# Zero matmuls ahead of the first km units instead of the first k'v, in a fused attention and channel-mix kernel with a new instruction table

## Chip, core and metric

The kernel runs on one core of one Trainium2 chip. The metric is the time of one execution on the device in microseconds (us), median of three runs. Beside it stands one profiled execution, whose trace gives the start and length of every instruction.

## The reference

Linear attention without softmax, a norm per head, and then a channel mix of RWKV kind (8 batches, 8 heads, 576 tokens, head width 64, model width 512, hidden width 1024):

```python
kv  = einsum('bhsd,bhse->bhde', k, v)          # k'v: one 64x64 matrix for each head
out = einsum('bhsd,bhde->bhse', q, kv)
out = out / sqrt(mean(out * out, -1) + 1e-6) * g_norm
x   = out.transpose(0, 2, 1, 3).reshape(B, S, 512)
xk  = mu_k * x + (1 - mu_k) * x_prev            # x_prev: the token before
xr  = mu_r * x + (1 - mu_r) * x_prev
k   = relu(xk @ w_k);  v = (k * k) @ w_v
return sigmoid(xr @ w_r) * v                    # [8, 576, 512], float32
```

## The kernel before

Everything runs in bf16 with sums in float32. The work of a batch is a string of units, each a handful of matmuls with what moves their result out of PSUM. The units are written out by hand in a table, `ORDER` (lines 18 to 113): eight periods of words, which the last loop of the kernel issues one after the other. A word is the unit's name, its arguments, a prime if VectorE instead of ScalarE does the elementwise part, and after `=` the PSUM banks (0 to 7) that the unit takes. Since each engine works through its own instructions in the order of issue, the table sets the order on every engine; an engine waits where an operand isn't there yet.

The units that the change and the prediction speak of:

- `wm.n`: n zero matmuls of 512 columns into a bank that nobody reads (`warm`, line 256). Twelve more are issued ahead of the table (line 629).
- `cast`: k and v of batch 0, first half of the heads, from float32. `kvc`, `qtc`, `uc`, `sqc`, `msc`, `rsc`, `mcc` (and `kvco`, `qtco`, which move out): batch 0 in a transposed form: k'v, q turned, q times k'v, its square, the mean over a head by a matmul, the root, the product that gives x.
- `kvh`, `qt`, `uh`, `sqh`, `redh`, `rsh`, `mulh`, `xh`, `x0h`: the same for batch 1 in halves of the heads; here the mean is a VectorE reduction and x is turned back by PE.
- `kv`, `qt`, `u`, `sq`, `red`, `nw` (eight small Newton steps on VectorE), `mul`, `x` and `x0` (the flips by PE), `xo` and `x0o` (their move out): batches 2 to 7.
- `wrap`, `dif`, `sc`, `add`, `fu`: x minus the token before, times mu, plus x; `add.b.0.*` gives xk, `add.b.1.*` gives xr.
- `Ka`, `Kz`, `Kp` and `K`: km, that is xk @ w_k and the relu. `Ka` and `Kz` are the two halves of the heads of batch 0's tokens 256 to 575, one block of 128 hidden columns each; `Kp.0.1.n` its tokens 0 to 255. `ks`, `ksp`: the squares.
- `R`: xr @ w_r and the sigmoid, for 128 tokens. `V` (or `Vq`, a quarter): the product with w_v for 128 tokens. `fin`: sigmoid times that, and the store. `L`: the last tile in two halves.
- `ld.i.b`: load of k, v or q (i = 0, 1, 2) of batch b, issued from GpSimd's queue. There is one buffer for each of the three, so the load of a batch's k waits until the k'v of the batch before has read it. The stores go out from SP's queue.

w_k comes in two halves of 512 hidden columns (`load_w`, line 195), issued ahead of the table on GpSimd's queue together with batch 1's inputs, w_v and w_r; `Ka.0.0` to `Ka.0.3` need the first half only.

Of the kernel before, what the change touches and what calls it, by code (L numbers as in the profile page):

```python
# [29 lines left out]
    mulh.1.0.0 mulh.1.1.0 Kp.0.1.2=5 Vq.0.3.0=4 Vq.0.3.1 mulh.2.0.0 rsh.5.9.0 mulh.0.0.0 Vq.0.2.0=3 Vq.0.2.1  # L30
    mulh.0.1.0 xh.0.2.0=51 xho.0.2.0.0 qt.1.1=20 qto.1.1.0 xho.0.2.0.1' qto.1.1.1' xh.2.2.0=76 xho.2.2.0.0
    x0h.0=51 x0ho.0.0 kvh.1=20 kvho.1.1 xho.2.2.0.1' ksp.0.1.4.8' kvho.1.0' Vq.0.1.0=6 x0ho.0.1' add.0.1.1
    uh.0.1=75 uh.1.1=02 sqh.0.0.1 sqh.0.1.1 redh.5.9.1 sqh.1.1.1 uh.2.1=1 sqh.2.0.1 Vq.0.1.1 sqh.1.0.1
    redh.0.5.1 Vq.0.3.2 rsh.5.9.1 rsh.0.5.1 mulh.0.1.1 mulh.0.0.1 Vq.0.2.2 Vq.0.2.3 mulh.1.0.1 Vq.0.1.2 tab
    Vq.0.3.3 Vq.0.0.0=5 mulh.1.1.1 mulh.2.0.1 Vq.0.0.1 xh.2.2.1=70 xho.2.2.1.0 xh.0.2.1=21 xho.0.2.1.1'
    xho.2.2.1.1' wrap.1 Vq.0.0.2 Vq.0.0.3 dif.1.384.576 sc.1.0.0.384.576' x0h.1=71 sc.1.0.2.384.576' x0ho.1.0
    x0ho.1.1' xho.0.2.1.0 dif.1.0.384 sc.1.0.1.384.576 sc.1.0.3.384.576 sc.1.0.2.0.384' R.0.0=0 sc.1.1.3'
    sc.1.0.0.0.384' ld.0.2 R.0.1=7 adda.1.0.384.576 R.0.2=2 sc.1.0.1.0.384' add.1.0.0.0.384 ld.1.2 Vq.0.1.3
    fin.0.0 fin.0.1 fin.0.2 R.0.3=1 sc.1.0.3.0.384 fin.0.3 add.1.0.1.0.384 sc.1.1.2
# [15 lines left out]
    K.2.0.0=7 K.2.0.1=2 K.2.1.0=5 K.2.1.1=7 K.2.2.0=2 K.2.2.1=5 K.2.3.0=7 K.2.3.1=2 K.2.4.0=5 red.3.5.9 nw.3.0.1
    add.2.1.1 K.2.4.1=7 nw.3.1.2 ks.2.0' K.2.5.0'=2 K.2.5.1=5 ks.2.1 K.2.6.0=7 K.2.6.1=2 nw.3.2.3 nw.3.3.4
    nw.3.4.5 nw.3.5.6 nw.3.6.7 ks.2.6 nw.3.7.8 mul.3.0.1 ld.1.4 ld.2.4 mul.3.2.0 mul.3.1.1 ks.2.4' ks.2.3 ks.2.2
    R.2.0=5 R.2.1=7 mul.3.0.0 V.1.8.0=2 V.1.8.1 mul.3.1.0 fin.1.8 K.2.7.0=3 qt.4.0=46 qto.4.0.0' x0.3=15
    x.3.0.4=70 xo.3.0.4.1' qt.4.1=23 x0o.3.0 ks.2.5' x0o.3.1 wrap.3 qto.4.0.1' kv.4=14 xo.3.0.4.0 K.2.7.1=5
# [7 lines left out]
    nw.4.7.8 mul.4.1.1 K.3.5.0=0 K.3.5.1=6 K.3.6.0=5 ld.2.5 mul.4.0.0 mul.4.2.0 add.3.1.1 mul.4.1.0 K.3.6.1=3
    ks.3.3 ks.3.6' ks.3.4 qt.5.1=04 kv.5=76 kvo.5.0' kvo.5.1 qto.5.1.1' qt.5.0=53 qto.5.0.0 add.3.1.0 qto.5.0.1'
    qto.5.1.0 ks.3.0 V.2.3.0=1 K.3.7.0=7 K.3.7.1=4 V.2.3.1 ks.3.2' R.3.4=6 ks.3.1' mul.4.0.1 fin.2.3 x0.4=53
    x.4.0.4=07 x0o.4.0' x0o.4.1 u.5.1=42 u.5.0=15 ks.3.7' xo.4.0.4.0 xo.4.0.4.1' wrap.4 ks.3.5' sq.5.1.0 dif.4  # L70
    u.5.2=6 sc.4.1.3' sc.4.0.2' ld.0.6 sc.4.0.3' R.3.5=3 V.3.5.0=7 sq.5.2.0 add.4.0.1 sc.4.0.1' sq.5.1.1
# [7 lines left out]
    V.3.7.0=5 ks.4.0' V.3.7.1 fin.3.7 ks.4.3 x0.5=34 x.5.0.4=27 x0o.5.0 x0o.5.1' kv.6=61 qt.6.0=03 xo.5.0.4.1'
    xo.5.0.4.0 kvo.6.0 wrap.5 kvo.6.1' qt.6.1=54 qto.6.1.1 qto.6.0.0 qto.6.1.0' dif.5 sc.5.0.3' K.4.6.0'=7  # L80
    qto.6.0.1 K.4.6.1=2 K.4.7.0=1 K.4.7.1=6 u.6.1=54 sc.5.0.2' sc.5.0.0 sc.5.0.1' ks.4.4' add.5.0.0 u.6.0=03
    u.6.2=2 sq.6.1.1 sq.6.0.1 sq.6.1.0 ld.0.7 add.5.0.1 sq.6.2.0 sc.5.1.0' V.3.8.0=1 V.3.8.1 sq.6.0.0 fin.3.8
    red.6.0.5 red.6.5.9 nw.6.0.1 nw.6.1.2 nw.6.2.3 nw.6.3.4 nw.6.4.5 ks.4.5 nw.6.5.6 nw.6.6.7 nw.6.7.8 R.4.0=7
# [3 lines left out]
    K.5.0.0=7 K.5.0.1=6 mul.6.2.0 mul.6.1.1 sc.5.1.1 K.5.1.0=1 K.5.1.1=7 R.4.3=6 ks.4.1 add.5.1.0 K.5.2.0=1
    K.5.2.1=7 K.5.3.0=2 K.5.3.1=6 K.5.4.0=4 ks.4.6 V.4.0.0=1 mul.6.1.0 mul.6.0.1 x0.6=72 x0o.6.1 mul.6.0.0
    ks.4.7' x0o.6.0' ld.1.7 kv.7=56 ld.2.7 kvo.7.1 sc.5.1.3' x.6.0.4=34 qt.7.1=07 qto.7.1.1 qt.7.0=26 qto.7.0.1'
    qto.7.0.0' V.4.0.1 sc.5.1.2' V.4.1.0=7 V.4.1.1 add.5.1.1 xo.6.0.4.1 wrap.6 xo.6.0.4.0 dif.6 kvo.7.0'  # L90
# [665 lines left out]
```

## Time and profile before

| | us |
|---|---|
| median of 3 runs | 204.84 (204.07, 204.84, 206.48) |
| the profiled execution, its time | 205.55 |
| the profiled execution, its span | 203.7 |
| PE (TensorE) busy in the span | 194.9 |
| VectorE (DVE) busy | 163.0 |
| ScalarE (ACT) busy | 135.8 |

The span runs from the first to the last instruction that the profile shows; about 1.9 us of the execution lie outside it. Busy time of PE counts matmuls, and their ends are modelled, so a busy PE is not a PE at its peak; PEld is the loading of weights beside it. PEclk is the clock that was granted to PE, 1.00 being full. In rows of the timeline the first number is the start, the second the length, and the bracket at the end says how long the engine sat idle before and what it waited for.

### The profile page before, as it was taken

How to read it: one execution, taken by the hardware profiler on the slowest of the kernel's cores; microseconds unless marked ns; L12 is line 12 of the kernel's file. 1: busy time of each engine (PE TensorE's matmuls, PEld its weight loads, DVE VectorE, ACT ScalarE, POOL GpSimd, SP SyncE). 2: the span in 40 equal slices, each digit the busy share in tenths (PEclk: the TensorE clock that was granted, in tenths of full speed). 3: DMA queues.
4: the chain of work that ended last, by engine and by line, in shares of the span. 5: the costliest groups of instructions: out<-in, count | busy, mean ns of one | idle time of the engine just before them, and what ended most of it. 6: DMA issues, size and time to landing. Idle time of an engine off the chain costs nothing.

```text
span 203.7 us, 6357 instructions
## 1 busy us (share of the span) xinstructions
PE 194.9 (96%) x2684; PEld 117.3 (58%) x2684; DVE 163.0 (80%) x359; ACT 135.8 (67%) x282; POOL 27.3 (13%) x44
## 2 busy tenths in 40 slices
PE   7969999999979999999999999999999999999992
...
DVE  1389899899969899979999999978898897467151
...
PEclk9996999999999999999999999999999999999999
DMA  6999999989989902995698339900440060006664
GB/s 214 214 205 206 202 205 171 204 156 178 247 115 206 282 5 55 139 214 154 98 226 172 69 56 188 211 5 3 105 103 3 0 156 3 0 0 156 138 141 136
DMA packets 21424, 27.22 MB, mean 134 GB/s; under 512 B 1804, under 2 KB 16404, under 8 KB 21396
## 3 DMA queue, kind: packets, MB, share of 16 engines
...
q8 instruction: 21, 0.34, 0.7%
q10 hardware_dynamic: 320, 0.39, 0.6%
q14 instruction: 7, 0.06, 0.1%
...
## 4 chain that ended last, share of the span: by engine, by line
PE 71%; DMA 21%; issue 3%; POOL 2%; DVE 0%; POOLq 0%
PE ps_v L605 27%; PE ps_km L573 25%; PE ps_r L595 11%; DMA in_k<-in_k_dram 7%; DMA in_q<-in_q_dram 6%; DMA in_v<-in_v_dram 5%; DMA q<-in_q_dram 3%; PE ps_qt L299 2%; PE ps_u L321 2%; PE ps_kv L285 2%; PE ps_x L377 2%; PE ps_v L613 1%; POOL q L185 0%; POOL wv_sb L204 0%; POOL in_k L193 0%
## 5 line engine op out<-in xcount | busy, mean ns | idle before, releaser
L605 PE MATMUL ps_v<-wv_sb,sqk 128*128 128x512 bf16 x280 | 66.1, 379 | 0.0
L573 PE MATMUL ps_km<-xk,wk_sb 128*128 128x288 bf16 (+3 forms) x480 | 63.4, 285 | 0.0
L573 PEld LDWEIGHTS <-wk_sb 128*128 128x128 bf16 x480 | 45.9, 98 | 15.8
L565 ACT ACTIVATE rt<-ps_km 128x288 bf16<-128x288 f32 (+3 forms) x92 | 37.4, 431 | 15.0 <-PE ps_km L573 9.5
L605 PEld LDWEIGHTS <-sqk 128*128 128x128 bf16 x280 | 26.5, 98 | 28.5
L598 ACT ACTIVATE sig<-ps_r 128x512 bf16<-128x512 f32 x36 | 21.0, 603 | 21.5 <-PE ps_r L595 21.3
L595 PE MATMUL ps_r<-wr_sb,xr 128*128 128x512 bf16 x144 | 34.4, 379 | 0.0
L618 DVE TENSOR_TENSOR out_sb<-ps_v,sig 128x512 f32<-128x512 f32 (+1 forms) x37 | 24.1, 671 | 11.2 <-ACT sig L598 4.4
L595 PEld LDWEIGHTS <-xr 128*128 128x128 bf16 x144 | 13.9, 98 | 15.2
L579 ACT ACTIVATE sqk<-rt 128x576 bf16<-128x576 bf16 (+1 forms) x27 | 18.3, 693 | 3.5 <-DVE rt L567 3.4
L543 ACT ACTIVATE m<-dx,cols 128x576 bf16<-128x576 bf16 (+2 forms) x25 | 17.5, 737 | 3.0 <-DVE dx L537 3.0
L567 DVE TENSOR_SCALAR rt<-ps_km 128x288 bf16<-128x288 f32 (+2 forms) x28 | 12.8, 461 | 7.4 <-PE ps_km L573 6.6
L362 DVE TENSOR_TENSOR y<-ps_u,rs 128x512 bf16<-128x512 f32 (+1 forms) x30 | 17.4, 629 | 0.3
L326 ACT ACTIVATE sq<-ps_u 128x512 bf16<-128x512 f32 (+1 forms) x30 | 14.6, 571 | 4.3 <-PE ps_u L321 4.3
L330 DVE TENSOR_REDUCE ss<-sq 128x16 f32<-128x1024 bf16 (+1 forms) x12 | 15.8, 1343 | 0.4 <-ACT sq L326 0.4
L193 POOL DMA_DIRECT2D in_k<-in_k_dram x6 | 4.5, 743 | 84.5 <-PE ps_kv L285 64.9
L581 DVE TENSOR_TENSOR sqk<-rt 128x576 bf16<-128x576 bf16 (+4 forms) x30 | 15.1, 512 | 0.1
L367 ACT ACTIVATE xT<-ps_x,cols 128x1024 bf16<-128x1024 bf16 (+3 forms) x19 | 11.9, 659 | 3.9 <-PE ps_x L377 3.8
L545 DVE TENSOR_SCALAR m<-dx,cols 128x576 bf16<-128x576 bf16 (+3 forms) x41 | 13.5, 354 | 0.2
L560 DVE TENSOR_TENSOR xr<-m,xT 128x1152 bf16<-128x1152 bf16 x16 | 11.9, 750 | 0.6 <-ACT m L543 0.6
L537 DVE TENSOR_TENSOR dx<-xT 128x2304 bf16<-128x2304 bf16 (+5 forms) x13 | 11.6, 891 | 0.6 <-ACT xT L367 0.3
L217 DVE COPY qT<-ps_qt 128x576 bf16<-128x576 bf16 x19 | 8.2, 451 | 4.2 <-PE ps_qt L299 3.0
...
## 6 DMA issues: line engine op xcount, KB each, us to landing
...
in_k<-in_k_dram POOLq DMA_DIRECT2D x6, 576.0 KB, 5.9
in_v<-in_v_dram POOLq DMA_DIRECT2D x6, 576.0 KB, 9.4
in_q<-in_q_dram POOLq DMA_DIRECT2D x6, 576.0 KB, 11.7
...
sqk<-in_k_dram SPq DMA_DIRECT2D x1, 576.0 KB, 3.8
...
sqk<-in_v_dram SPq DMA_DIRECT2D x1, 576.0 KB, 4.7
```

The source lines that it names most:

```text
L326: ACT.activation(out=sq[:, rg(t0, n, i) if n else slice(0, 1)], in_=held["u", a, part, i][1], func=AF.Square)
L330: DVE.tensor_reduce(out=ss[:, g0:g1], in_=sq[:, g0:g1], op=ALU.add, axis=AX.X)
L362: DVE.tensor_mul(out=y[:, g], in0=give(("u", a, part, i)), in1=rs[:, g].unsqueeze(3).to_broadcast([128, max(n, 1), NHP, HD]))
L543: eng.activation(out=out_, in_=in_, func=AF.Copy, scale=mu)
L565: eng.activation(out=dst, in_=ps, func=AF.Relu)
L573: nc.tensor.matmul(ps[:, n, :], wk_sb[:, cc, 128 * fc:128 * fc + 128], at[b]["xk"][:, cc, c0:c1], start=(cc == 0), stop=(cc == NHP - 1))
L579: eng.activation(out=sqk[:, fcs, o:o + n], in_=src, func=AF.Square)
L581: eng.tensor_mul(out=sqk[:, fcs, o:o + n], in0=src, in1=src)
L595: nc.tensor.matmul(ps, xr[:, cc, 128 * t:128 * t + 128], wr_sb[:, cc, :], start=(cc == 0), stop=(cc == NHP - 1))
L598: ACT.activation(out=sig[b, t], in_=give("r"), func=AF.Sigmoid)
L605: nc.tensor.matmul(ps, sqk[:, fc, 128 * t:128 * t + 128], wv_sb[:, fc, :], start=(fc == 0), stop=(fc == NFC - 1))
L618: DVE.tensor_mul(out=o, in0=give(key), in1=sig[b, t][:, c])
```

## The change

The zero matmuls of the table are placed elsewhere, and the whole table is written anew: the order of units, the engine of many elementwise parts, and the banks. Nothing is added to or taken from the computation. The twelve zero matmuls ahead of the table stay. In the table there were 4, 2 and 2 ahead of the first k'v (`kvc.0.2`), 4 behind q's first turn and 1 at the very end; now there are 2 ahead of the first k'v, 2 behind q's first turn, 2 ahead of each of the last three means or their squares (`msc.3`, `msc.4`, `msc.5`), 1 behind the first km unit (`Ka.0.3`), and 1 at the end. In period 1 the turns of batch 3's q (`qt.3`) move behind five `V` units.

```diff
 ORDER = (
     """
-    cast.1' wm.4=1 cast.0 wm.2=2 wm.2=3 kvc.0.2=45 kvco.1 qtc.0.2=67 qtco.0 wm.4=0 kvco.0' uc.0=1 qtco.1'
-    qtc.2.2=23 sqc.0 qtco.2' uc.1=4 sqc.1 msc.0=5 qtco.3' rsc.0 cols=7 mcc.0 msc.1=6 kvc.2.1=0 kvco.2 uc.4=2
-    uc.2=3 kvc.3.1=7 rsc.1 sqc.2 msc.2=5 mcc.1 rsc.2 kvco.3' uc.5=0 uc.3=1 sqc.3 msc.3=6 difh.0.0.256.576
-    sc.0.0.1.256.576' sqc.4 msc.4=4 mcc.2 rsc.3 sc.0.0.0.256.576' sqc.5 dih.0.2.256.576 add.0.0.0.256.576
-    Ka.0.0=7 mcc.3 rsc.4 fu.0.0.2.256.576 dih.0.3.256.576 wrap.0 msc.5=5 rsc.5 Ka.0.2=3 Ka.0.1=6
...
-    Ka.0.4=1 sc.0.1.0' Kz.0.4' ksp.0.0.4.8' sc.0.1.2' sc.0.1.1 Kp.0.1.0=2 qt.1.0=73 sc.0.1.3' Kp.0.1.1=6
...
+    wm.2.0=1 cast.1' cast.0 kvc.0.2=23 kvco.0' qtc.0.2=45 kvco.1' wm.2.1=6 qtco.0' uc.0=7 qtco.1' uc.1=0
+    qtc.2.2=12 sqc.0 msc.0=3 qtco.2' sqc.1 cols=4 msc.1=6 rsc.0 rsc.1 kvc.2.1=5 kvco.2 uc.2=1 uc.4=4 qtco.3
+    mcc.0 mcc.1 difh.0.0.256.576 sc.0.0.0.256.576' sc.0.0.1.256.576' add.0.0.0.256.576 sqc.2 kvc.3.1=3 kvco.3
+    msc.2=6 rsc.2 mcc.2 dih.0.2.256.576 fu.0.0.2.256.576 uc.3=5 uc.5=7 sqc.3 sqc.4 wm.2.2=2 msc.3=0 wm.2.4=3
+    rsc.3 msc.4=6 mcc.3 dih.0.3.256.576 wrap.0 fu.0.0.3.256.576 wm.2.3=2 sqc.5 msc.5=1 rsc.5 Ka.0.3=3 mcc.5
+    wm.1.5=0 rsc.4 mcc.4 Ka.0.2=2 Ka.0.1=5 difh.0.0.0.256 Ka.0.0=1 fu.0.0.0.0.256 Kz.0.3 Kz.0.1 sc.0.1.0
+    fu.0.0.1.0.256 difh.0.1.0.256 Kz.0.2 Kz.0.0 Ka.0.7=0 Kz.0.7 fu.0.0.3.0.256 Ka.0.6=6 Kz.0.6 Ka.0.5=7
+    fu.0.0.2.0.256 sc.0.1.2 sc.0.1.1' Ka.0.4=4 Kz.0.4' add.0.1.0 Kz.0.5 ksp.0.0.4.8 Kp.0.1.0'=3 Kp.0.1.1=5
...
     """,
     """
-    Kp.1.0.0'=0 sc.1.1.0 sc.1.1.1 add.1.1.0 kv.2=72 kvo.2.0 Kp.1.0.1=5 Kp.1.0.2=1 add.1.1.1 Kp.1.0.3=6
...
-    Kp.1.1.7=6 ld.1.3 kv.3=51 ld.2.3 mul.2.1.0 mul.2.0.0 mul.2.1.1 x0.2=27 mul.2.0.1 x.2.0.4=03 kvo.3.1 x0o.2.1'
-    ksp.1.1.4.6 xo.2.0.4.0 qt.3.1=46 qto.3.1.1 qt.3.0=17 x0o.2.0' xo.2.0.4.1' V.1.6.0=2 qto.3.0.1' ksp.1.1.6.8'
...
+    Kp.1.0.0'=5 Kp.1.0.1=0 Kp.1.0.2=7 fin.0.1 sc.1.1.1' sc.1.0.2.0.384' sc.1.1.0' add.1.1.0 sc.1.0.0.0.384'
+    add.1.0.0.0.384 sc.1.0.3.0.384 add.1.0.1.0.384 sc.1.1.2' Kp.1.0.3=3 kv.2=25 ld.0.3 kvo.2.1' Vq.0.3.3 R.0.3=4
+    Kp.1.1.0=0 ld.1.3 Kp.1.1.1=7 qt.2.0=35 qt.2.1=40 ksp.1.0.0.8' qto.2.1.1' qto.2.0.1 qto.2.1.0 kvo.2.0
...
+    ksp.1.1.2.4 Kp.1.1.4=1 Kp.1.1.5=5 Kp.1.1.6=6 Kp.1.1.7=0 kv.3=13 ksp.1.1.6.8 mul.2.1.1 mul.2.0.1 x.2.0.4=56
+    mul.2.2.0 x0.2=70 x0o.2.0 kvo.3.0 V.1.5.0=4 ksp.1.1.4.6 V.1.7.0=2 xo.2.0.4.1' wrap.2 V.1.4.0=7 xo.2.0.4.0'
+    V.1.4.1 x0o.2.1' V.1.5.1 dif.2 sc.2.0.0' sc.2.0.3 sc.2.1.3 qt.3.0=16 qto.3.0.1 sc.2.1.1 qto.3.0.0 fin.1.4
...
     """,
...
-    K.5.4.1=6 K.5.5.0=2 K.5.5.1'=4 ks.5.1 sc.6.0.1 sc.6.0.3' qto.7.1.0' ks.5.0 sc.6.1.2 fin.4.0 fin.4.1 ks.5.2'
...
+    kv.7=72 kvo.7.0 mul.6.0.1 qto.7.1.0' qto.7.1.1' x.6.0.4=53 xo.6.0.4.1' x0.6=10 x0o.6.0 x0o.6.1' fin.4.1
+    xo.6.0.4.0 wrap.6 dif.6 sc.6.0.1' sc.6.0.2 sc.6.0.3' sc.6.0.0' R.5.4=6 ks.5.4 add.6.0.1 V.4.2.0=7 V.4.2.1
+    add.6.0.0 V.4.3.0=1 ks.5.0' V.4.3.1 ks.5.3' ks.5.5' qt.7.0=30 qto.7.0.0 qto.7.0.1 K.5.7.0=5 K.5.7.1=4
     """,
     """
...
+    K.6.0.0'=6 K.6.0.1'=3 K.6.1.0=0 fin.4.2 K.6.1.1'=5 K.6.2.0=4 ks.5.7' K.6.2.1=6 kvo.7.1' fin.4.3 K.6.3.0=3
...
@@ -715,7 +714,7 @@
-        "wm": lambda eng, n: warm(n),
+        "wm": lambda eng, n, *place: warm(n),
```

`place` is not used by the code; it only makes the words differ.

More of the change, by code (lines that the diff above doesn't have):

```diff
@@ L30 @@
[L30 to L39, printed above, removed]
@@ L52 @@
-    add.2.1.0
-    """,
-    """
[L55 to L59, printed above, removed]
@@ L67 @@
[L67 to L71, printed above, removed]
@@ L79 @@
[L79 to L83, printed above, removed]
@@ L84 @@
-    R.4.1=6 R.4.2=1
-    """,
-    """
[L87 to L90, printed above, removed]
-    K.5.4.1=6 K.5.5.0=2 K.5.5.1'=4 ks.5.1 sc.6.0.1 sc.6.0.3' qto.7.1.0' ks.5.0 sc.6.1.2 fin.4.0 fin.4.1 ks.5.2'
@@ new lines @@
+    nw.3.0.1 nw.3.1.2 K.2.3.0=7 K.2.3.1=2 nw.3.2.3 nw.3.3.4 K.2.4.0=1 R.2.0=7 K.2.4.1'=2 K.2.5.0=1 nw.3.4.5
+    ks.2.3' ld.0.4 ld.1.4 K.2.5.1'=7 K.2.6.0=2 K.2.6.1=1 V.1.8.0=7 ks.2.6 ks.2.4 nw.3.5.6 nw.3.6.7 R.2.1=2
+    nw.3.7.8 ks.2.0' K.2.7.0=1 mul.3.2.0 V.1.8.1 mul.3.1.1 K.2.7.1=4 ks.2.7 x0.3=62 mul.3.0.0 x0o.3.1 ks.2.1'
+    mul.3.1.0 kv.4=51 mul.3.0.1 x.3.0.4=30 xo.3.0.4.1 fin.1.8 x0o.3.0' kvo.4.1' ks.2.2' ld.2.4 qt.4.0=47
+    qto.4.0.1' ks.2.5 qto.4.0.0 xo.3.0.4.0' wrap.3 dif.3 sc.3.0.0' qt.4.1=61 V.2.1.0=2 R.2.2=7 sc.3.0.3'
@@ new lines @@
+    kvo.4.0' qto.4.1.1' sc.3.0.2 qto.4.1.0 sc.3.1.2' sc.3.0.1' V.2.0.0=0 V.2.2.0=3 ld.0.5 ld.1.5 V.2.0.1
+    add.3.0.0 V.2.1.1 sc.3.1.1 fin.2.0 u.4.1=47 u.4.0=51 sq.4.1.0 add.3.0.1 u.4.2=6 sq.4.2.0 sq.4.0.0 V.2.2.1
+    fin.2.1 fin.2.2 sq.4.0.1 red.4.5.9
+    """,
+    """
+    K.3.0.0=0 sq.4.1.1 K.3.0.1=2 K.3.1.0=3 red.4.0.5 nw.4.0.1 K.3.1.1=0 K.3.2.0=2 K.3.2.1=3 K.3.3.0=0 K.3.3.1=2
+    K.3.4.0=3 K.3.4.1=0 ld.2.5 nw.4.1.2 ks.3.2 nw.4.2.3 K.3.5.0=2 K.3.5.1=3 nw.4.3.4 nw.4.4.5 nw.4.5.6 K.3.6.0=0
@@ new lines @@
+    nw.4.6.7 ks.3.4 nw.4.7.8 mul.4.2.0 R.2.3=6 K.3.6.1=2 mul.4.0.1 mul.4.1.0 kv.5=13 mul.4.1.1 kvo.5.1 mul.4.0.0
+    sc.3.1.3' x0.4=40 qt.5.1=75 x0o.4.0 sc.3.1.0' add.3.1.0 qt.5.0=62 qto.5.0.1' ks.3.6 K.3.7.0=3 ld.0.6
+    K.3.7.1=4 qto.5.1.1 V.2.3.0=2 V.2.3.1 kvo.5.0 ks.3.1' x0o.4.1 ks.3.3' qto.5.1.0' x.4.0.4=34 qto.5.0.0
+    u.5.1=75 ks.3.0' add.3.1.1 ks.3.5 fin.2.3 ks.3.7 xo.4.0.4.1' wrap.4 u.5.0=10 sq.5.1.1 sq.5.0.0 sq.5.0.1
+    xo.4.0.4.0' dif.4 red.5.5.9 u.5.2=6 sq.5.2.0 R.3.4=2 R.3.5=4 V.3.4.0=3 V.3.4.1 sc.4.0.2 sc.4.1.0 sq.5.1.0
```

83 lines of the change are left out of this document (46 added, 37 removed).

## The prediction

> **What bounds the kernel now.** I read the page first: who is busy, and in which slices of the span.
>
> ```profile
> PE 194.9 (96%) x2684; PEld 117.3 (58%) x2684; DVE 163.0 (80%) x359; ACT 135.8 (67%) x282; POOL 27.3 (13%) x44
> ...
> PE   7969999999979999999999999999999999999992
> ...
> DVE  1389899899969899979999999978898897467151
> ...
> PEclk9996999999999999999999999999999999999999
> DMA  6999999989989902995698339900440060006664
> ```
>
> PE is the engine that is full. Two slices are not: the third (10 to 15 us) and the twelfth (56 to 61 us). In the fourth PEclk reads 6: PE is busy there, at a lower clock. VectorE is nearly as full as PE over most of the span, and the DMA engines are full in most of the first eleven slices. So PE sets the end, but before 60 us it may wait for VectorE or a load. The windows put numbers on it; after busy PE come PEclk, the DMA share and GB/s as the last three columns.
>
> ```profile
> 10.00:15.00 5.00, 3.48 (x56) 1.74 (x54) 4.31 (x12) 4.23 (x11) 2.79 (x4) 1.00 1.23 206
> 15.00:20.00 5.00, 4.74 (x23) 2.88 (x24) 4.89 (x13) 2.87 (x7) 1.97 (x3) 0.66 1.22 206
> ...
> 60.00:70.00 10.00, 10.00 (x93) 5.64 (x91) 9.24 (x19) 6.49 (x13) 0.59 (x1) 1.00 1.18 240
> ...
> 190.00:200.00 10.00, 9.95 (x54) 5.10 (x52) 3.33 (x6) 1.79 (x3) 0.00 (x0) 1.00 0.65 153
> ```
>
> The twelve rows between the last two all show PE busy for 10.00 of 10. So from 60 us on the end is a plain sum of matmuls: what PE gains before that comes through, and nothing can be gained after. What there is to gain shows in the half-microsecond windows and in the waits of PE:
>
> ```profile
> 15.50:16.00 0.50, 0.50 (x3) 0.28 (x2) 0.50 (x2) 0.34 (x1) 0.50 (x1) 0.50 1.25 209
> ...
> 18.50:19.00 0.50, 0.50 (x4) 0.31 (x3) 0.46 (x3) 0.39 (x2) 0.20 (x1) 0.79 1.20 205
> ```
>
> ```profile
> PE ps_qt L299 <- DMA in_q<-in_q_dram: 1.2, 1, 1.2
> ...
> PE ps_ms L446 <- ACT sq L440: 0.9, 2, 0.6
> ...
> PE ps_km L645 <- DMA wk_sb<-in_moe_w_k_dram: 0.5, 1, 0.5
> ```
>
> The granted clock was 0.50 from about 15.3 to 18.7 us, right behind the stretch in which PE had 1.5 us of idle time in five. The longest wait is 1.2 us for a load of q. The timeline gives the steps of the start:
>
> ```profile
> 1.20 6.38 PE L259 MATMUL ps_warm<-zeros 128*128 128x512 bf16 x20 [1.20 <-DVE eps L222]
> ...
> 6.02 0.76 DVE L217 CAST rt<-sqk 128x1152 bf16<-128x1152 f32 x1 [4.43 <-DMA sqk<-in_v_dram]
> 7.51 0.48 PE L414 MATMUL ps_kv<-rt 64*64 64x64 bf16 x36
> ...
> 9.24 0.35 PE L435 MATMUL ps_u<-qT,kv 64*64 64x384 bf16 x2
> ...
> 15.26 0.69 PE L645 MATMUL ps_km<-xk,wk_sb 128*128 128x320 bf16 x2 [0.51 <-DMA wk_sb<-in_moe_w_k_dram]
> ...
> 16.07 5.54 PE L645 MATMUL ps_km<-xk,wk_sb 128*128 128x320 bf16 x30
> ...
> 17.99 0.71 POOL L204 DMA_DIRECT2D wv_sb<-in_moe_w_v_dram  x1 [1.83 <-DMA wk_sb<-in_moe_w_k_dram]
> ...
> 19.81 0.88 DVE L549 SCALAR_TENSOR_TENSOR xk<-dx,cols,xT 128x256 bf16<-128x256 bf16 x2
> ...
> 21.45 1.04 PE L573 MATMUL ps_km<-xk,wk_sb 128*128 128x256 bf16 x8
> ```
>
> **The change, part by part.** *Zero matmuls at the start.* Ahead of the first k'v stand 14 instead of 20. At full clock the last six cost 6 x 0.22 = 1.3 us (a quarter of the 0.86 for four 512-column matmuls, from the row of `V` below), so PE is free at 6.3; v's cast ends at 6.78, and k'v starts at about 6.85 instead of 7.51. Behind it two of them stand where four stood, and q's first move goes from ScalarE to VectorE, so the first u comes near 8.2 instead of 9.24. None of this moves the end by itself, since the first km unit cannot start before 15.2, when the first half of w_k lands: that transfer is the cover. It does bring VectorE's chain forward by up to 1.0: the last product for the second part of km, done at 20.69 in the trace, comes near 19.7. *Added:* two, two, two and one from the last three means to behind the first km unit, 7 x 0.22 = 1.5 us, into the 1.5 us that the row 10 to 15 leaves idle. Cost zero while the squares are as late as now; if that cover goes, at most 1.5. Over the whole kernel there are 24 zero matmuls instead of 25.
>
> *The clock.* Thirty 320-column matmuls took from 16.07 to 21.45, 179 ns each. By columns from the 0.86 us for four of 512 (below) they take 0.135 each at full clock. With the clock kept, the 16 that need only the first half of w_k end near 17.7 (with the one zero matmul between). The second half lands at 17.97 (the POOL row: its wait for w_k ends there), the other 16 end at 20.2, and the second part of km starts there instead of at 21.45: 1.25 us. Bounds: nothing, if the clock drops all the same, and 1.75, VectorE's limit (19.7). I take 1.25.
>
> On the half clock the Trainium skill ("TensorE: Matmul & The Clock Gate", section "HAM oscillation — how this bites in real kernels") says that the clock is kept as long as no idle gap exceeds about 3.4 us. The trace disagrees: the longest gap here was 0.60 and the clock fell. By the rule the added zero matmuls would buy nothing and 1.25 would be 0; by the row they can buy it.
>
> *From there to the first prefetched batches.* Up to 42 us VectorE is full, and loads follow each other: batch 2's wait for the last k'v of batch 1, batch 3's for that of batch 2.
>
> ```profile
> 30.48 0.54 PE L464 MATMUL ps_kv<-in_v,in_k 64*64 64x64 bf16 x36
> ...
> 32.09 0.75 POOL L193 DMA_DIRECT2D in_v<-in_v_dram  x1
> ...
> 41.95 0.77 PE L285 MATMUL ps_kv<-in_v,in_k 64*64 64x64 bf16 x72 [0.16 <-DMA in_v<-in_v_dram]
> ...
> 43.94 0.75 POOL L193 DMA_DIRECT2D in_v<-in_v_dram  x1
> ...
> 53.34 2.76 PE L573 MATMUL ps_km<-xk,wk_sb 128*128 128x384 bf16 x16
> ...
> 56.04 0.78 PE L285 MATMUL ps_kv<-in_v,in_k 64*64 64x64 bf16 x72
> ...
> 58.70 0.80 PE L299 MATMUL ps_qt<-ident,in_q 64*64 64x64 bf16 x72 [1.25 <-DMA in_q<-in_q_dram]
> ```
>
> ```profile
> in_v<-in_v_dram POOLq DMA_DIRECT2D x1, 576.0 KB, 9.7
> ...
> in_v<-in_v_dram POOLq DMA_DIRECT2D x1, 576.0 KB, 11.9
> ```
>
> Between the second part of km and `kvh.1` the new table has 0.7 us more of matmuls (two more `Vq` at 0.43 each, one flip fewer), so of the 1.25 about 0.6 to 0.9 is left there, and batch 2's loads start as much earlier. Batch 2's v landed at 32.09 + 9.7 = 41.8 and now lands near 41.0, and `kv.2` comes near 41.1 (0.85 earlier). From `kv.2` to `kv.3` the trace took 14.1. Three units of eight 192-column matmuls leave that stretch (by columns from the 384-column row 0.65 each), and a `Vq` and an `R` enter it (0.43 + 0.86): 13.4, so PE is at `kv.3` at 54.5. Batch 3's v, issued 0.85 earlier at 43.1, lands 11.9 later, at 55.0. So `kv.3` waits 0.5 and starts at 55.0: **1.0 earlier**. Bounds: nothing (the load lands when it did, the DMA being the limit) to 1.6 (PE's own 54.5). I take 1.0.
>
> *q of batch 3 moved back.* `qt.3` stood 1.5 us behind `kv.3` and waited for its load until 58.70. In the new table five `V` halves stand ahead of it (5 x 0.86 = 4.3), so PE reaches it near 60.7, where the load, in at 58.7 in the trace and issued 0.85 earlier now, is in near 57.9. The wait, 1.25 by the timeline, goes: **1.25 earlier**. Nothing else is late in its place: the V halves need squares that ScalarE makes before. Bounds: 1.0 to 1.25.
>
> *Order on POOL and SP.* The loads and the stores come in the same sequence in both tables, so no queue is passed; two stores of batch 0 move about 5 us back and still go out before batch 3's v lands.
>
> *The rest of the table.* From `kv.3` to the end both tables hold the same matmuls, 141.5 us. What can be lost is PE waiting at the head of a batch: flip, move out, difference, scale, add, then the first K. The prices:
>
> ```profile
> 59.50 5.29 PE ps_v L605 x24
> ...
> 89.52 6.37 PE ps_km L573 x52
> ```
>
> ```profile
> L560 DVE TENSOR_TENSOR xk<-m,xT 128x1152 bf16<-128x1152 bf16 x12 | 8.9, 753 | 0.5 <-ACT m L543 0.4
> L537 DVE TENSOR_TENSOR dx<-xT 128x2304 bf16<-128x2304 bf16 x6 | 8.1, 1352 | 0.4 <-ACT xT L367 0.3
> L545 DVE TENSOR_SCALAR m<-dx,cols 128x576 bf16<-128x576 bf16 x34 | 11.7, 366 | 0.1
> L618 DVE TENSOR_TENSOR out_sb<-ps_v,sig 128x512 f32<-128x512 f32 x35 | 23.2, 685 | 9.7 <-ACT sig L598 4.4 <-PE ps_v L605 3.7 <-issue 1.3
> L369 DVE TENSOR_SCALAR xT<-ps_x,cols 128x1024 bf16<-128x1024 bf16 x5 | 3.7, 747 | 0.8 <-PE ps_x L377 0.8
> ```
>
> A unit of four 512-column matmuls is 5.29/6 = 0.88 at most, 0.86 over long stretches; a K 6.37/13 = 0.49. Batch 6 in the new table: between flip and `K.6.0.0` PE has one R, four V, one qt and two K, 0.86 + 3.44 + 0.40 + 0.98 = 5.7, with the small flip 5.8. VectorE meanwhile has one move (0.75), a small one (0.28), a `fin` (0.69), wrap (0.22), difference (1.35), three scales (1.10) and two adds (1.51): 5.9, or about 5.3, since in the timeline neighbours on VectorE overlap by some 0.06. It fits or just doesn't. The same sums, PE against VectorE with the overlap, for batches 2, 3, 4 and 7: 6.9 to 6.3, 7.75 to 7.8, 12.1 to 12.7, 7.3 to 7.6; in the table before 8.6 to 7.0, 8.55 to 6.4, 9.5 to 8.7, 9.85 to 9.0, and for batch 6 12.05 to 9.0. The margins are thinner. Some of VectorE's work counted here can run before the flip ends, so I take 0.3 in all; bounds 0 and 4.9 (without the overlap, 1.0 more in each: 0.4 + 1.1 + 1.6 + 0.5 + 1.3).
>
> **Sum.** -1.0 - 1.25 + 0.3 = -2.0 (rounded). The profiled execution's 205.55 (span 203.7) becomes 203.6. It lies 0.7 above the median of the three runs shown; the mean of these four executions is 205.2, and 2.0 less is **203.2**. Within 1% is 202.8 to 206.9, about what a measurement of this kernel can tell from no change.
>
> **Rivals.** *A, the clock falls all the same* (12%). For it: seven zero matmuls fill 1.5 us, and the squares now come earlier, so PE may idle elsewhere; against it: that stretch then is almost full. The 1.25 at km is lost, `kv.3` gains 0.2, q's wait goes and 0.3 is lost later: 205.2 - 1.15 = 204.0. *B, the wait changes its load* (10%): the slices show the DMA engines full nearly all the way to 55 us, so v of batch 3 may land at 55.85 as before. Only the 1.25 is won, with 0.3 lost: 204.3. Against it is one window, with a DMA share of 0.37: the queue does run dry between batches.
>
> ```profile
> 42.00:43.00 1.00, 1.00 (x77) 0.96 (x78) 1.00 (x3) 1.00 (x3) 0.00 (x0) 1.00 0.37 61
> ```
>
> *C, more is won* (20%): v lands with PE at 54.5, no stall at the heads: -1.55 - 1.25 = -2.8, 202.4. *D, slower* (16%): VectorE arrives late at the batch heads, at five of them by the shortfalls above. The point from which it decides: VectorE more than 0.5 us behind at the end of a batch's flip. 4.9 instead of 0.3: 205.2 - 2.25 + 4.9 = 207.9. For it: the thinner margins and VectorE's 80%; against it: the table before ran stretches where VectorE had 5 us more work than PE (from `R.3.4` to the end of batch 5's Newton steps) without one PE wait. On the clock's own schedule the Trainium skill ("TensorE: Matmul & The Clock Gate", section "What's actually happening") says that the windows run freely, not from the kernel's start; so A can hold in one execution and not in the next, which no single profile shows.
>
> **How the numbers follow.** Forecast 42%, A 12%, B 10%, C 20%, D 16%. Beyond 1% faster: two fifths of the forecast (202.8 is 0.4 from it) and nine tenths of C, 0.35. Beyond 1% slower: D nearly whole, 0.15. Within: 0.50. Range: C with its spread gives 201.6; above, A and B and the milder part of D reach 206.6. D's own value stays outside.
>
> **What would show it.** Right: PEclk 9 in the fourth slice; the second part of km at 20.2; `kv.2` near 41.1; `kv.3` near 55.0 with a wait for in_v of up to 0.5; no wait for in_q; windows of 10.00 from 60 us on; the last matmul near 197.8. Wrong: PE waiting for VectorE at the first K of a batch (xk), or half clock at any km unit.

## The result, and the profile after

| | before | after |
|---|---|---|
| median of 20 runs each | 205.05 (204.07 to 206.48) | 203.91 (203.48 to 206.91) |
| the profiled execution, its time | 205.55 | 203.60 |
| its span | 203.7 | 201.8 |

The ratio is 0.9936, 95% interval 0.9911 to 0.996. (Ratios leave out executions that lie more than 1.5% above the fastest of their kernel; medians hold all.) The forecast was 203.2: the time lies in its range, 0.7 above it. The medians differ by 1.1 and the two profiled executions by 1.9, where 2.0 was forecast. Two of the steps came out otherwise, and they nearly cancel.

First the page of after: the same rows as before.

```profile
PE 194.5 (96%) x2683; PEld 116.6 (58%) x2683; DVE 164.2 (81%) x360; ACT 134.6 (67%) x281; POOL 27.2 (13%) x44
...
PE   7989999999999999999999999999999999999990
...
PEclk9999999999999999999999999999999999999999
```

The two thin slices of PE have filled (the third from 6 to 8, the twelfth from 7 to 9), and the fourth PEclk slice reads 9 instead of 6. The last slice of PE, though, fell from 2 to 0: PE ends earlier than the span by more than it did. The windows (busy time of each engine, then PEclk, DMA share, GB/s) and the waits of PE say the same in numbers.

```profile
10.00:15.00 5.00, 4.42 (x59) 2.28 (x59) 4.55 (x12) 4.57 (x11) 2.80 (x4) 1.00 1.24 206
15.00:20.00 5.00, 4.98 (x36) 3.52 (x36) 4.86 (x13) 3.91 (x10) 2.14 (x3) 1.00 1.21 206
...
190.00:200.00 10.00, 6.85 (x40) 3.71 (x38) 2.83 (x5) 2.39 (x4) 0.00 (x0) 1.00 0.75 170
```

```profile
PE ps_warm L258 <- DVE eps L221: 1.2, 1, 1.2
PE ps_u L434 <- DVE xT L453: 0.3, 1, 0.3
PE ps_kv L413 <- DMA rt<-in_v_dram: 0.2, 1, 0.2
PE ps_qt L422 <- DMA q<-in_q_dram: 0.2, 1, 0.2
```

No wait for the squares, for w_k or for q of batch 3 is left, and none at the head of a batch. PE's own steps, from the timeline (start, length; line numbers are one lower than before):

```profile
6.94 0.48 PE L413 MATMUL ps_kv<-rt 64*64 64x64 bf16 x36
...
8.61 0.71 PE L434 MATMUL ps_u<-qT,kv 64*64 64x384 bf16 x4
...
15.19 0.43 PE L644 MATMUL ps_km<-xk,wk_sb 128*128 128x320 bf16 x2
...
15.67 4.24 PE L644 MATMUL ps_km<-xk,wk_sb 128*128 128x320 bf16 x30
19.75 2.04 PE L572 MATMUL ps_km<-xk,wk_sb 128*128 128x256 bf16 x16
...
40.77 0.78 PE L284 MATMUL ps_kv<-in_v,in_k 64*64 64x64 bf16 x72
...
54.41 0.78 PE L284 MATMUL ps_kv<-in_v,in_k 64*64 64x64 bf16 x72
...
60.20 0.80 PE L298 MATMUL ps_qt<-ident,in_q 64*64 64x64 bf16 x72
...
194.73 1.91 PE L612 MATMUL ps_v<-wv_sb,sqk 128*128 128x256 bf16 x16
```

The last row is the last tile, `L`. Before, it started at 197.82 (below): PE got there 3.1 us sooner, of which 1.6 had been won at `kv.3` (56.04 to 54.41) and 1.5 from there on (197.82 - 56.04 = 141.8; 194.73 - 54.41 = 140.3). The span is only 1.9 shorter. What is missing, 1.2, lies behind that row: from the start of `L` to the end of the span it was 203.7 - 197.82 = 5.9 and is 201.8 - 194.73 = 7.1. The end of before, and then of after (ACTq is the store issue on ScalarE's own queue, `sig` the sigmoid of the last tile, DVE its product):

```profile
197.07 0.56 ACTq L621 DMA_DIRECT2D out_dram<-out_sb  x1
197.82 1.91 PE L613 MATMUL ps_v<-wv_sb,sqk 128*128 128x256 bf16 x16
198.02 0.60 ACT L598 ACTIVATE sig<-ps_r 128x512 bf16<-128x512 f32 x1 [4.58 <-PE ps_r L595]
```

```profile
193.69 2.67 ACTq L620 DMA_DIRECT2D out_dram<-out_sb  x1
196.41 0.60 ACT L597 ACTIVATE sig<-ps_r 128x512 bf16<-128x512 f32 x1 [2.61 <-PE ps_v L612]
197.04 0.76 DVE L617 TENSOR_TENSOR out_sb<-ps_v,sig 128x256 f32<-128x256 f32 x2 [2.22 <-ACT sig L597]
```

Before, the store of tile 7.6 took ScalarE's queue for 0.56 and the sigmoid started 0.2 after `L`. After, the same store held the queue for 2.67, the sigmoid started 1.7 after `L`, and both products, which the last stores wait for, came behind it. Nothing in the table asked for that.

### The profile page after: what moved, and what is told of

Its sections match the earlier page's. It is cut to its first block, busy times and chain, and to the rows that moved or that the text cites. A ratio compares the mean times of both kernels' runs of the same rounds, so it can differ in the third digit from the quotient of the medians.

```text
span 201.8 us, 6347 instructions
## 1 busy us (share of the span) xinstructions
PE 194.5 (96%) x2683; PEld 116.6 (58%) x2683; DVE 164.2 (81%) x360; ACT 134.6 (67%) x281; POOL 27.2 (13%) x44
## 3 DMA queue, kind: packets, MB, share of 16 engines
q1 hardware_dynamic: 6164, 10.23, 18.7%
## 4 chain that ended last, share of the span: by engine, by line
PE 87%; DMA 4%; DVE 2%; POOL 1%; issue 1%; ACT 1%; ACTq 1%; DVEq 0%; POOLq 0%
PE ps_v L604 30%; PE ps_km L572 28%; PE ps_r L594 15%; DMA rt<-in_v_dram 4%; PE ps_qt L298 3%; PE ps_x L376 2%; PE ps_u L320 2%; PE ps_km L644 2%; PE ps_kv L284 2%; PE ps_warm L258 1%; ACTq L620 1%; POOL q L184 1%; ACT sq L486 1%; DVE sqk L580 1%; POOL rt L184 1%
## 5 line engine op out<-in xcount | busy, mean ns | idle before, releaser
L604 PE MATMUL ps_v<-wv_sb,sqk 128*128 128x512 bf16 x280 | 67.1, 379 | 0.3
L572 PE MATMUL ps_km<-xk,wk_sb 128*128 128x288 bf16 (+3 forms) x480 | 64.6, 285 | 0.0
L564 ACT ACTIVATE rt<-ps_km 128x288 bf16<-128x288 f32 (+3 forms) x93 | 38.5, 431 | 25.2 <-PE ps_km L572 22.1
L578 ACT ACTIVATE sqk<-rt 128x576 bf16<-128x576 bf16 (+2 forms) x27 | 19.5, 730 | 0.2
L542 ACT ACTIVATE m<-dx,cols 128x576 bf16<-128x576 bf16 (+1 forms) x22 | 16.6, 777 | 4.2 <-DVE dx L536 4.2
L580 DVE TENSOR_TENSOR sqk<-rt 128x576 bf16<-128x576 bf16 (+3 forms) x30 | 14.4, 494 | 3.1 <-ACT rt L564 2.9
L566 DVE TENSOR_SCALAR rt<-ps_km 128x288 bf16<-128x288 f32 (+3 forms) x27 | 12.3, 466 | 5.3 <-PE ps_km L572 5.3
L544 DVE TENSOR_SCALAR m<-dx,cols 128x576 bf16<-128x576 bf16 (+3 forms) x44 | 14.6, 357 | 0.2
L366 ACT ACTIVATE xT<-ps_x,cols 128x128 bf16<-128x128 bf16 (+3 forms) x17 | 9.1, 563 | 5.0 <-PE ps_x L376 4.9
L559 DVE TENSOR_TENSOR xr<-m,xT 128x1152 bf16<-128x1152 bf16 x16 | 11.9, 751 | 0.2
L559 DVE TENSOR_TENSOR xk<-m,xT 128x1152 bf16<-128x1152 bf16 (+2 forms) x16 | 10.9, 699 | 0.3
```

Of the source, the lines that this page charges most:

```text
L542: eng.activation(out=out_, in_=in_, func=AF.Copy, scale=mu)
L559: DVE.tensor_add(out=dst, in0=m[:, hs, c0:c1], in1=x[:, hs, c0:c1])
L564: eng.activation(out=dst, in_=ps, func=AF.Relu)
L572: nc.tensor.matmul(ps[:, n, :], wk_sb[:, cc, 128 * fc:128 * fc + 128], at[b]["xk"][:, cc, c0:c1], start=(cc == 0), stop=(cc == NHP - 1))
L578: eng.activation(out=sqk[:, fcs, o:o + n], in_=src, func=AF.Square)
L580: eng.tensor_mul(out=sqk[:, fcs, o:o + n], in0=src, in1=src)
```

## The experiments

**1. Is it the zero matmuls that keep the clock?** `after_nofill` takes the seven of them out, `after_lead` puts six back ahead of the first k'v, and `before_fill` puts seven into the old table.

```diff
 after_nofill (the table after)
-  ... sqc.4 wm.2.2=2 msc.3=0 wm.2.4=3 / fu.0.0.3.256.576 wm.2.3=2 sqc.5 / wm.1.5=0 rsc.4
+  ... sqc.4 msc.3=0 / fu.0.0.3.256.576 sqc.5 / rsc.4
 after_lead (the table after)
-    wm.2.0=1 cast.1' cast.0
+    wm.8.0=1 cast.1' cast.0
 before_fill (the table before)
-  sqc.3 msc.3=6 / sc.0.0.1.256.576' sqc.4 / Ka.0.0=7 mcc.3 / wrap.0 msc.5=5
+  sqc.3 wm.2 msc.3=6 / sc.0.0.1.256.576' wm.2 sqc.4 / Ka.0.0=7 wm.1 mcc.3 / wrap.0 wm.2 msc.5=5
```

> The changed kernel without the seven zero matmuls between the fourth mean and the first km unit. If they keep the clock (my theory): PEclk falls to 0.5 for about 3.4 us from near 15 us, the second part of km starts at 20.5 to 21.5 instead of 19.75, kv.3 comes 0.3 to 1.0 later than 54.4, and the time is 0.3 to 1.0 above the changed kernel (204.2 to 204.9). Rival, the fillers buy nothing (the clock holds through gaps this short, or PE was not the limit there): PEclk stays 1.00, the second part of km starts at 19.75 or earlier, the time is 203.6 to 204.0.

> The changed kernel with twenty zero matmuls ahead of the first k'v, as before, instead of fourteen. My theory is that the shorter lead is covered by the landing of w_k: the first k'v starts near 8.2 instead of 6.94, but the first km unit still near 15.2 to 15.6 and the second part of km within 0.4 of 19.75; time within 0.3 of the changed kernel's. Rival, the earlier start is what the change wins: the second part of km starts 0.8 to 1.2 later, and the time is 0.5 to 1.2 above the changed kernel's.

> The kernel before with seven zero matmuls put in at the matching places (two ahead of each of msc.3, msc.4 and msc.5, one behind the first Ka), nothing else. My theory: the clock stays 1.00 and the second part of km starts 0.8 to 1.3 earlier (20.2 to 20.7), but the wait for batch 3's q at qt.3 takes most of it back, since those loads are limited by DMA: end 0 to 0.5 earlier, time 204.5 to 205.1. Rival, the fillers alone are the gain: qt.3 comes 1.0 earlier as well and the time is 203.7 to 204.1, the same as the changed kernel's.

Measured: `after_nofill` 204.82, 0.9 above after (ratio to before 0.9992, 0.9956 to 1.0027, which just overlaps that of after); `after_lead` 204.17 (0.9962, 0.9921 to 1.0002); `before_fill` 205.82 (1.0048, 1.0006 to 1.009), a miss, and slower than before. The window from 15 to 20 us of the first and the last, and the first km units of `after_nofill`:

```profile
15.00:20.00 5.00, 5.00 (x26) 3.11 (x26) 4.86 (x13) 2.92 (x7) 2.09 (x3) 0.68 1.22 206
```

```profile
15.00:20.00 5.00, 4.99 (x34) 3.25 (x35) 4.80 (x12) 3.73 (x10) 2.14 (x3) 1.00 1.21 206
```

```profile
15.18 6.00 PE L644 MATMUL ps_km<-xk,wk_sb 128*128 128x320 bf16 x32
21.02 1.15 PE L572 MATMUL ps_km<-xk,wk_sb 128*128 128x256 bf16 x9
```

Without them the clock is 0.68 again and the second part of km starts at 21.02 instead of 19.75; with them, in either table, it is 1.00. A profile is one execution, and the mean clock of every execution is on record. In the profiles a fall lasts 3.4 us at half clock (15.3 to 18.7 in before), and half of 3.4 in 204 is 0.008, so an execution with a fall has a mean of 0.992 or less. A mean just above that needs no fall under load: in after the clock falls only behind the last matmul (0.87 from 199 us to the end).

| | executions | with a fall |
|---|---|---|
| old table without the seven (before, `before_qt`, `before_qt2`) | 133 | 56 |
| old table with them (`before_fill`, and `before_fill_qt` and `before_fill_qt2` below) | 36 | 2 |
| new table without them (`after_nofill`) | 12 | 3 |
| new table with them (after, `after_lead`, and the four of experiment 4) | 74 | 8 |

So in the old table the zero matmuls do keep the clock. In the new one 3 of 12 are too few to tell. There the seven are worth 0.9 in the median, but that this is the clock is shown for the profile only: the nine executions of `after_nofill` without a fall still have a median of 204.49, against 203.75 for the 17 such of after. (The profiled one, 206.00, reached `kv.3` 1.15 later than after did, and PE lost another 1.13 in one gap at 78.8 us for which the profile shows no releaser.)

The longest gap of PE in the 3.4 us ahead of the fall was 0.7 in `after_nofill`. That speaks against the 3.4 us of the Trainium skill that the prediction weighed ("TensorE: Matmul & The Clock Gate", "HAM oscillation — how this bites in real kernels"); the next section of that page, "A second HAM failure mode: psum-queue depth-cycling", says that short idle times, if frequent enough, drop the clock too, and the trace fits that. How full PE was does not settle it alone: `before_qt` and `before_qt2` (below) are the same up to there, PE was busy 3.56 and 3.57 of the 5 us ahead, and the clock fell in the one and not in the other. The six zero matmuls ahead of the first k'v make 0.3 in the median, which is within the noise; km starts 0.5 later (15.68), so the start is not all cover.

In the old table the kept clock bought nothing: the eleven executions of `before_fill` without a fall have a median of 205.79, the 68 of before 204.50. That it is even slower stays open. In its profile it reaches the second part of km 0.9 sooner (20.52), but `kv.3` only 0.3 sooner, where it waits for its load, and q's load is waited for as before:

```profile
55.73 0.77 PE L285 MATMUL ps_kv<-in_v,in_k 64*64 64x64 bf16 x72 [0.31 <-DMA in_v<-in_v_dram]
...
58.48 0.80 PE L299 MATMUL ps_qt<-ident,in_q 64*64 64x64 bf16 x72 [1.34 <-DMA in_q<-in_q_dram]
```

**2. Is the move of q's turns worth its 1.25?** In the old table alone, with the zero matmuls as well, and then once more with a second move beside it.

```diff
 before_qt (the table before); before_fill_qt is the same on before_fill
-  qt.3.1=46 qto.3.1.1 qt.3.0=17 x0o.2.0' ... V.1.6.0=2 ... V.1.4.0=3 V.1.4.1 ... V.1.5.0=7 V.1.6.1
+  x0o.2.0' ... V.1.6.0=2 ... V.1.4.0=3 V.1.4.1 ... V.1.5.0=7 V.1.6.1 qt.3.1=46 qto.3.1.1 qt.3.0=10 ...
 before_qt2 (the table before); before_fill_qt2 is the same on before_fill
-  qt.3.1=46 qto.3.1.1 qt.3.0=17 x0o.2.0' ... V.1.6.0=2 ... V.1.4.0=3 ... sc.2.0.0' kvo.3.0' u.3.1=06
+  x0o.2.0' ... V.1.6.0=2 kvo.3.0' ... V.1.4.0=3 qt.3.1=46 qto.3.1.1 qt.3.0=17 ... sc.2.0.0' u.3.1=06
```

> The kernel before with batch 3's q turned five V units later, nothing else. My theory: the wait of 1.2 for in_q goes, qt.3 starts near 61.8 without a wait, the last matmul comes 1.0 to 1.3 earlier and the time is 203.7 to 204.1. Rival, the wait only moves to u.3 or to the first K of batch 2, since q's moves out and the scales now share ScalarE: 204.6 to 205.2.

> The kernel before with the seven zero matmuls and with batch 3's q turned five V units later. Theory: the zero matmuls win 0.9 at the second part of km and 0.3 at kv.3, and with q's wait gone this reaches the end: 1.2 to 1.6 earlier, 203.4 to 203.9, 0.2 to 0.5 below the same without the zero matmuls. Rival, the zero matmuls cost as much as they win, as they did alone: no difference between the two.

> The table before, with q's turns of batch 3 behind two V halves instead of five, and with the second move out of batch 3's k'v issued ahead of q's moves, so that u.3 need not wait for it. Theory (the wait for q is worth its 1.25 us, and the first attempt lost it only because VectorE's queue held k'v's move behind q's): no wait for in_q, none at u.3, the last tile 1.0 to 1.25 us earlier than before, 203.8 to 204.1. Rival (the order before has no slack on VectorE there, so a wait turns up at the next place that needs it, u.3 or the first K of batch 2): not below the kernel before, 205.0 to 206.0.

> The same, with the seven zero matmuls of the filled start as well. Theory (the clock's gain was taken back by the waits for the two loads): the wait for batch 3's v stays, 0.3 to 0.9, the wait for q is gone, kv.3 0.3 earlier than before; last tile about 1.5 us earlier than before, 203.4 to 203.8. Rival: as above, 205.0 to 206.3.

Measured: `before_qt` 206.10 (1.008, 1.0045 to 1.0116), `before_fill_qt` 206.29 (1.0077, 1.0041 to 1.0112): both slower, both misses. The waits of PE in `before_qt`:

```profile
PE ps_u L321 <- DVE kv L217: 1.4, 1, 1.4
```

q's wait was gone and a longer one had come: u.3 needs the second half of batch 3's k'v moved out, and that move stood on VectorE behind q's moves, which now came later. `before_qt2` puts it ahead of them, and q's turns behind two `V` halves instead of five; the two are not separated. Then neither wait is left, and the median is 204.38 against 205.00 (0.9972, 0.9936 to 1.0008): above the 203.8 to 204.1 expected, and not clear of no change. In its profile `L` starts at 196.66, 1.16 sooner than in that of before; but 0.43 of this was there at `kv.3` already (55.61), because in that execution the clock happened to be kept. Behind `kv.3` 0.73 of the 1.25 came through. The rival, a wait at the next place, did not come in that profile: PE waits for nothing from 56 us on. `before_fill_qt2` was to add the clock to that and took 204.86 (1.0014, 0.9977 to 1.005): a miss. Its row says why:

```profile
56.12 0.77 PE L285 MATMUL ps_kv<-in_v,in_k 64*64 64x64 bf16 x72 [0.81 <-DMA in_v<-in_v_dram]
```

PE was there at 55.3 and waited for v. In the old table the load lands at about the same time however early it is issued, between 55.1 and 56.6 in its six kernels: 43.94 + 11.9 = 55.8 in before, 43.01 + 12.6 = 55.6 in `before_fill`, 42.93 + 13.1 = 56.0 here. That was rival B. In after it lands at 42.75 + 9.7 = 52.5 (the issue in the timeline of after, and its row among the DMA issues):

```profile
42.75 0.76 POOL L192 DMA_DIRECT2D in_v<-in_v_dram  x1
```

```profile
in_v<-in_v_dram POOLq DMA_DIRECT2D x1, 576.0 KB, 9.7
```

But for the next load of k at 55.5, the issues between 42 and 56 us differ in one thing, the stores of the output, first before, then after:

```profile
out_dram<-out_sb SPq DMA_DIRECT2D x8, 128.0 KB, 3.4
```

```profile
out_dram<-out_sb SPq DMA_DIRECT2D x4, 128.0 KB
```

Seven or eight stores go out beside the load in all six kernels with the old table, four in after. But the number of stores does not settle it. With the new table the load took 9.3 to 9.7 in five kernels (four or five stores) and 10.6 in `after_sp7` (four), but 11.5 in `after_nofill` (six) and in `after_qtfwd` (experiment 3), whose rows these are:

```profile
out_dram<-out_sb SPq DMA_DIRECT2D x5, 128.0 KB, 4.1
in_v<-in_v_dram POOLq DMA_DIRECT2D x1, 576.0 KB, 11.5
```

That the stores are what makes the load late is a guess from the rows and not shown; no run moved the stores alone.

**3. The same move undone in the new table, for the first of q's two turns.**

```diff
 after_qtfwd (the table after)
-  x0o.2.0 kvo.3.0 V.1.5.0=4 ... V.1.7.0=2 ... V.1.4.0=7 ... sc.2.1.3 qt.3.0=16 qto.3.0.1 sc.2.1.1 qto.3.0.0
+  x0o.2.0 kvo.3.0 qt.3.0=42 qto.3.0.1 qto.3.0.0 V.1.4.0=7 V.1.5.0=4 ... V.1.7.0=2 ... sc.2.1.3 sc.2.1.1
```

> The table after, with the first turn of batch 3's q brought forward ahead of the five V halves, right behind the flips of batch 2. Theory (in the new order q comes in at 45.48 + 11.0 = 56.5, PE gets there at 55.8): a wait of 0.7 for in_q, all of it lost, 0.7 above the kernel after, 204.6. Rival (the move of q's turns is worth nothing in the new order, because q is now in early enough or VectorE sets the head of batch 2): same as the kernel after, 203.9.

Measured: 206.28 (ratio 1.0027, 0.9978 to 1.0075), 2.4 above after instead of 0.7. The twelve executions fall into two groups. Five lie above 208, all with a mean clock of 0.992 or less; the other seven, at 0.994 or more, have a median of 205.39, 1.5 above after. The profiled execution, 208.67, is one of the five:

```profile
58.57 0.48 PE L298 MATMUL ps_qt<-ident,in_q 64*64 64x64 bf16 x36 [2.26 <-DMA in_q<-in_q_dram]
```

```profile
60.00:65.00 5.00, 4.65 (x15) 1.72 (x14) 0.22 (x2) 3.04 (x5) 0.00 (x0) 0.66 0.98 166
```

q landed at 58.5, not 56.5 (issued at 45.95, and 12.6 under way instead of 11.0), so PE waited 2.26; and behind that gap the clock fell to 0.66 for the next five microseconds, which costs 1.7 (0.34 x 5). With 0.5 that it was behind at `kv.3` already and a wait of 0.35 for q's move out, that is nearly all of the 5.1 between the spans. So in the new table the late place of q's turns is worth more than the load's time in after says: it covers the load where it is late, and with it the clock.

**4. The tail.** Three ways around the long store: `after_tail` puts the last R, and so its sigmoid, ahead of the store; `after_sp` and `after_sp7` send the second store of tile 7.6 over SP's queue (`after_sp` that of 7.7 too). And one that leaves the stores alone, `after_shift`.

```diff
 after_tail
-    V.7.7.1 fin.7.6 R.7.8=0 fin.7.7 L.0=7 L.1=5 wm.1=6
+    V.7.7.1 R.7.8=0 fin.7.6 fin.7.7 L.0=7 L.1=5 wm.1=6
 after_sp7 (after_sp: nc.sync for both, always)
-  queues=(nc.sync, nc.scalar if b == B - 1 and t > 5 else nc.sync)
+  queues=(nc.sync, nc.scalar if b == B - 1 and t > 6 else nc.sync)
 after_shift
     DVE.memset(eps, 1e-6)
+    for _ in range(8):
+        ACT.copy(out=idle_cell, in_=eps)
```

> The changed kernel with R.7.8 issued ahead of fin.7.6, so that the sigmoid of the last tile stands ahead of ScalarE's first store. If that sigmoid is late because ScalarE's queue is held by the store (2.67 us in the profile of the changed kernel): it starts about 0.1 after the last R's matmuls, 1.6 earlier than now, the stretch from the last matmul to the end shrinks from 5.2 to 4.0, and the time is 0.7 to 1.2 below the changed kernel's (202.7 to 203.2). Rival, the long store was an accident of one execution: the time is within 0.3 of the changed kernel's.

> The changed kernel with all stores of the full tiles on SP's queue (ScalarE's queue keeps only the second halves of the last tile's two stores). If ScalarE's first store holds its queue for 2.6 us and so the last sigmoid back by 1.6: the sigmoid starts about 0.1 behind the last R's matmuls, the stretch from the last matmul to the end shrinks from 5.2 to 4.0-4.5, time 0.5 to 1.1 below the changed kernel's (202.8 to 203.4). Rival, the stores are limited by the DMA engines whatever queue issues them: the stretch stays above 5.0 and the time within 0.3.

> The changed kernel with tile 6's second store on SP's queue and tile 7's still on ScalarE's, which stands behind the last sigmoid. If it is the store ahead of the sigmoid that costs: the same sigmoid time as with all on SP, and the end at most 0.3 from it. If any first store on ScalarE's queue takes 2.6 us here, the last tile's stores behind it are late and the end stays within 0.3 of the changed kernel's.

> The table after unchanged; eight copies of one column are added on ScalarE at the start, where it waits for k from 2.0 to 4.6 us. Their result is not used. Theory (the 2.67 us store issue of the kernel after is ScalarE waiting for its next instructions: an instruction packet of 8 KB falls at ScalarE's 319th or 320th recorded instruction in every kernel here, and in the kernel after that is the store ahead of the last sigmoid): with eight more instructions in front, the packet falls some eight instructions sooner, near 182 to 191 us, where nobody waits for ScalarE; the store issue of tile 7.6 is near 0.56, the last sigmoid follows R at once, about 1.2 below the kernel after, 202.7. Rival (the long issue belongs to the store itself, to what other transfers are under way or to its place ahead of the last tile): it stays above 2 us and the time that of the kernel after, 203.9.

Measured: `after_tail` 203.77 (0.996, 0.9923 to 0.9997); `after_sp` 202.78 (0.9918, 0.9879 to 0.9957); `after_sp7` **202.62** (0.9921, 0.9884 to 0.9957); `after_shift` **202.70** (0.9907, 0.9873 to 0.994). `after_tail` gained next to nothing, a miss. In its profile the sigmoid came at once (195.60), but all four of ScalarE's stores now stand behind it, the first takes 1.34 and the last issue ends only at 199.2; from the start of `L` (195.41) to the end it is 6.6, where after has 7.1 and before 5.9. In `after_sp7` the sigmoid follows `L` by 0.2 again, 1.6 sooner than in after:

```profile
194.64 1.91 PE L612 MATMUL ps_v<-wv_sb,sqk 128*128 128x256 bf16 x16
```

```profile
194.84 0.60 ACT L597 ACTIVATE sig<-ps_r 128x512 bf16<-128x512 f32 x1 [1.13 <-PE ps_r L594]
```

So the missing 1.2 is the long store, shown. Why it was long: the queue q14 carries instructions, in packets of 8 KB. Late in the span one such packet falls at ScalarE's 317th to 320th recorded instruction, in the profiles of all fourteen kernels. In before that is at 183.6, and ScalarE still has 20 instructions to go; the new table gives ScalarE eight instructions fewer, and there it is the store at 193.69. In the three other kernels with this end and this count (`after_nofill`, `after_lead`, `after_qtfwd`) the same store took 2.64 to 2.73. Window 194.5 to 195 of after:

```profile
q14 instruction: 1, 0.01, 5.0%
```

`after_shift` puts eight useless instructions in front, at a time when ScalarE waits for k, and changes nothing else:

```profile
2.04 1.75 ACT L224 COPY idle_cell<-eps 128x1 f32<-128x1 f32 x8
```

```profile
193.79 0.56 ACTq L623 DMA_DIRECT2D out_dram<-out_sb  x1
195.02 0.60 ACT L600 ACTIVATE sig<-ps_r 128x512 bf16<-128x512 f32 x1 [1.13 <-PE ps_r L597]
```

The packet now falls at 185.3, where nobody waits, the same store takes 0.56, and the kernel 202.70. The rival, that the store itself is slow, is out. Either remedy makes a kernel that beats both, by 1.2 to 1.3 against after in the medians. The ratios to before overlap, because before itself spreads; the times hardly do: the six of `after_shift` lie from 202.65 to 202.80 and eleven of the twelve of `after_sp7` below 203.4, where the shortest of the twenty of after is 203.48.

## Why the prediction was right, and where it was not

| step | predicted | measured in after |
|---|---|---|
| first k'v; first u | 6.85; 8.2 | 6.94; 8.61 |
| clock from 15 to 20 us | kept | 1.00 |
| second part of km | 20.2 | 19.75 |
| `kv.2` | 41.1 | 40.77 |
| v of batch 3 lands | 55.0 | 52.5 |
| `kv.3` | 55.0 behind a wait of 0.5 | 54.41, no wait |
| `qt.3` | near 60.7, no wait | 60.20, no wait |
| waits at the heads of batches | 0.3 | none |
| end of the last matmul | 197.8 | 196.6 (`L`) |
| behind the last matmul | unchanged | 1.2 more |

Right in the profile of after: the clock is kept, q's wait is gone (experiment 3 shows what it costs to undo that), and no stall came at the heads (rival D: VectorE's margins were thin and held). That zero matmuls keep the clock is shown for the old table, not what it is worth in the new one. Mis-sized: the -1.0 at `kv.3` was -1.6. The step that failed is "Batch 3's v, issued 0.85 earlier at 43.1, lands 11.9 later": issued at 42.75, it took 9.7, so PE's own 54.5 was the limit, as in rival C. What brought v in is open. The prediction had dismissed the two stores that "move about 5 us back" as passing no queue; the rows of experiment 2 leave them possible, no more. In the old order the load takes the clock's gain back. With the +0.3 at the heads, which did not come, and 0.2 besides, PE gained 3.1 instead of 2.0.

Missed altogether: the end. The prediction took the tail as given because both tables hold the same units there. They do; but ScalarE's count of instructions ahead of them differs, and 1.2 was lost. -1.6 - 1.25 - 0.2 + 1.2 = -1.9 is the forecast's sum by errors of opposite sign, which is luck. Three slips in the working leave the sum as it is: by the 384-column row (2.76 for 16) eight 192-column matmuls are 0.69 and not 0.65; PE is busy for 142.7 from `kv.3` to the end of before, not 141.5; and batch 6 falls short by 5.9 - 5.8 = 0.1 without the overlap, not by 0.5, which lowers rival D's bound alone.

One thing about the base. The profile of before is an execution in which the clock fell, and not all do. Of 109 executions of before beside the experiments (one with a mean clock of 0.756 left out), 41 have a mean of 0.992 or less, so a fall, and a median of 206.09; 68 have 0.996 or more and 204.50. In after 3 of 20 have a fall (206.87 in the median), and the other 17 have 203.75. So about 0.75 of the 1.1 between the medians is there where no clock falls, and the rest goes with falls that are drawn less often (3 of 20 are few, and the 109 come from other sessions). The prediction took the clock's whole price off a base of four executions of which the profiled one had a fall; the pair of profiles, one with a fall and one without, shows 1.9, and the medians 1.1. That a fall can be drawn in one execution and not in the next the prediction had as a property of rival A, from the Trainium skill's free-running windows ("TensorE: Matmul & The Clock Gate", "What's actually happening"); the spread agrees with it, but it shows above all in the kernel before.
